# Moving six DMA transposes from the activation queue to the load queue, and the attention steps they feed, in a woven attention and MLP kernel

## The chip, the cores and the metric

The kernel runs on one core of a Trainium2 chip. The metric is the device time of one execution in microseconds (us), the median of several runs. The span in a profile, from the first to the last instruction, is some 1.8 us shorter than the time of the same run. TensorE (PE) multiplies matrices, VectorE (DVE), ScalarE (ACT) and GpSimd (POOL) work element by element, and SyncE (SP) mostly issues DMAs. ACT can issue DMAs too. A run is called slow when it lies over 1.5% above the fastest of its kernel; on one core there is no second die to confirm that, so the label only says that the run was long.

## The reference

The kernel computes, for 4 batches of 768 tokens, a linear attention with a decaying state (8 heads of 64) and then a low rank token mixer and an MLP of 512 to 2048 to 512.

```python
state = gamma * state + k[t] (outer) v[t]          # for each head and token
y[t]  = (q[t] @ state) / sqrt(64)
x     = y as (batch, 768, 512)
u     = x + (xT @ U @ V)T                          # U: 768 x 32, V: 32 x 768
out   = u + max(u @ w_ch1, 0) @ w_ch2              # 512x2048 and 2048x512
```

The recurrence is computed in chunks of 128 tokens: a score block, a causal mask, a mix with the values, and a running state.

## The kernel before

The kernel is one long program in a fixed order. After a prologue (the attention of batch 0) come four MLPs. Into the MLP of batch b−1, PE's main work, the attention of batch b is woven: each small step has a mark, a fraction of the MLP's estimated PE work, and is emitted when that mark is passed. The names in the profile: `in` are loaded tiles (in SBUF, the memory on the chip that the engines work from); POOL casts them to `qd`, `kd`, `vd`; `qT`, `kT` are transposes of pairs of chunks; DVE reorders `qT` to `qO`; a score `s` is kT times qO on PE; `a` is the masked score on DVE; mixes write `o`.

The transposes of batches 2 and 3 are done by DMA, and all loads go out from SP. An engine issues its DMAs one after the other, in the order of the program; I call these its queue. Which engine issues the transposes is this line:

```python
def turn_dma(nm, b, sc):
    (nc.sync if b > 2 else nc.scalar).dma_start_transpose(
        out=turned(nm, b, sc)..., in_=pre[nm, b, sc]...)
```

All loads go out from SP. They are not issued where they are used but 16 tiles ahead: the program starts with 16 loads, and each cast is followed by one further load, of the tile 16 places later in a fixed list.

```python
RING = 16
for _ in range(RING):
    feed_one()                       # nc.sync.dma_start of the next tile
...
def prep_keys(b, keys):
    for key in keys:
        src = take(*key)
        nc.gpsimd.tensor_tensor(t, src, g, op=ALU.mult)   # or tensor_copy for v
        feed_one()
```

The steps of batch 2 (`b == 2`), in the MLP of batch 1:

```python
for sc in range(b == 2, NSC):
    prep_keys(b, pair(b, sc))
if b == 2:
    at = [0.15 + 0.083 * i for i in range(NCK)]       # six chunks
    turns = [None, 0.02, 0.1, 0.19, 0.27, 0.36]       # transposes q k q k q k
lag = [0.0, 0.04, 0.1]                                # state, score, mix
if b == 2:
    for i, f in enumerate(w2_sums(4) + w2_sums(6)):   # differences of w2, DVE
        tracks.append(([f], 0.04 + 0.025 * i, ...))
...
for sc in range(NSC):
    d = at[2 * sc] + lag[1] - 0.02                    # qO just before its score
    tracks.append((q_order(b, sc) on DVE, d, d))
```

The same MLP also gives DVE the "g_sums": sums of halves of the activations `gT`, for a seven product form of the second matmul.

Of the kernel before, what the change touches and what calls it, by code (L numbers as in the profile page):

```python
# [9 lines left out]
fp32 = mybir.dt.float32  # L10
# [8 lines left out]
def kernel(  # L19
# [11 lines left out]
    nc = tc.nc  # L31
# [51 lines left out]
    def evac(eng, dst, src):  # L83
        if eng == "A":
            nc.scalar.activation(dst, src, AF.Copy)  # L85
        else:
            nc.vector.tensor_copy(out=dst, in_=src)  # L87
# [8 lines left out]
    Ub = wts.tile([P, NCK, RK], fp16)  # L96
    V4 = wts.tile([P, S], fp16)
    VR = NSC * RK
    Uf = wts.tile([P, NSC, 2, RK], fp32)
    Vf = wts.tile([VR, SC], fp32)  # L100
    Uh = wts.tile([P, NSC, 2, RK], fp16)
    Vh = wts.tile([VR, SC], fp16)
    w1b = wts.tile([P, NCB, DH], fp16)
    w2b = wts.tile([P, NM, DM], fp16)
    w2t = [wts.tile([P, NH, DQ], fp16, name=f"w2t{i}") for i in range(4)]
# [72 lines left out]
    nc.vector.memset(ones, 1.0)  # L178
    idle_bank = [None]

    def keep_busy(n, fresh=False):
        if fresh:
            idle_bank[0] = bank("mlp")
        for i in range(4 * n):
            nc.tensor.matmul(idle_bank[0][:, ts(i % 4, P)], ones[:, :P],  # L185
                             ones[:, :P], start=True, stop=True,
                             skip_group_check=True)
# [121 lines left out]
    def spread_u():  # L309
        u_p = bank("mlp")  # L310
        for x in range(2):
            for two in range(2):
                nc.tensor.matmul(u_p[ds(HP * two, HP), ds(NSC * RK * x, NSC * RK)],
                                 ident16[:, ds(HP * x, HP)], Uh[:, :, two],
                                 start=(x == 0), stop=True,
                                 skip_group_check=True)
        evac("A", Ub.rearrange("p (s x) r -> p x s r", x=2),
             u_p[:, :NCK * RK].rearrange("p (x s r) -> p x s r", x=2, s=NSC))

    def spread_v():  # L320
        v_p = [bank(t) for t in ("st", "qk")]
        for f in range(NSC):
            nc.tensor.matmul(v_p[f // 2][:, ts(f % 2, SC)], v_sel[:VR, f], Vh,
                             start=(f % 2 == 0), stop=True,
                             skip_group_check=True)
        evac("D", V4[:, :2 * SC], v_p[0])
        evac("A", V4[:, 2 * SC:], v_p[1][:, :SC])

    def prep_w1(mb):
# [105 lines left out]
    def turned(nm, b, sc):  # L435
        if (nm, b, sc) not in live:
            live[nm, b, sc] = rmid.tile([P, 2, 4, P], bf16, tag=nm + "T",
                                        bufs=2, name=f"{nm}T_{b}_{sc}")
        return live[nm, b, sc]

    def q_order(b, sc, src):
# [18 lines left out]
            evac("A", turned(nm, b, sc)[:, r], tp[:, r])  # L460

    def turn_dma(nm, b, sc):
        (nc.sync if b > 2 else nc.scalar).dma_start_transpose(
            out=turned(nm, b, sc).rearrange("p x n m -> p (x n) m"),
            in_=pre[nm, b, sc].rearrange("p x h d -> p (x h d)"))

# [120 lines left out]
    def part(f, *args):  # L587
        return lambda: f(*args)  # L588
# [252 lines left out]
    prep_pair("q", 0, "PD")  # L841
    for sc in range(NSC):
        last = sc + 1 == NSC
        keep_busy(3 if sc else 9, fresh=not last)
        turn_block("k", sc, "D")
        keep_busy(0 if sc else 7)
        turn_block("q", sc, "AD" if last else "A")
        prep_pair("v", sc, "PD" if last else "PA")
        if sc:
            state_half(sc - 1, 1)  # L850
        else:
            keep_busy(4)
        score_block(sc, 0)
        if last:
            prep_uv()
        else:
            prep_pair("k", sc + 1, "PD")
            prep_block("P", "q", sc + 1, 0)
            keep_busy(0 if sc else 3)
        if sc:  # L860
            score_block(sc, 1, "mlp", "DA")
        else:
            score_block(sc, 1)
        if last:
            state_half(sc, 0)
            mix_block(sc - 1, "AD")
            continue
        prep_block("D", "q", sc + 1, 1)
        if sc:
            mix_block(sc - 1, "AA")  # L870
        keep_busy(4 if sc else 1, fresh=sc > 0)
        state_half(sc, 0)
        if sc == 0:
            nc.vector.tensor_scalar(mask, t2.rearrange("p two m -> p (two m)"),
                                    srange, None, op0=ALU.is_ge)
    for mb in range(4):
        prep_w1(mb)
    spread_u()
    for c in range(2):
        x_turn(c, 0)  # L880
    mix_block(NSC - 1, "AD", ("s", "s"))
    spread_v()
    block_stack.close()
    gtp = ctx.enter_context(tc.tile_pool(name="gtp", bufs=1))
    outp = ctx.enter_context(tc.tile_pool(name="outp", bufs=6))
    lr_open(0)
    lr_proj(0)
    for c in range(2):
        x_turn(c, 2)
    for c in range(2, NCB):  # L890
        x_turn(c, 0)
        x_turn(c, 2)
    idle_bank[0] = bank("s")
# [13 lines left out]
    for b in range(1, B + 1):  # L907
# [10 lines left out]
        if b < B:  # L918
            if b == 1:
                at = [0.475, 0.575, 0.63, 0.69, 0.745, 0.8]  # L920
                lag = [0.01, 0.035, 0.065]
                for sc in range(NSC):
                    keys = pair(b, sc)
                    c0, c1 = 2 * sc, 2 * sc + 1
                    if sc:
                        tracks.append(([part(prep_keys, b, keys[:AHEAD])],
                                       at[c0] - 0.1, 1))
                    tracks.append(([part(prep_keys, b, keys[AHEAD:])],
                                   at[c1] - 0.1, 1))
                    for f, d in ((part(turn_pe, "q", b, sc), at[c0] - 0.025),  # L930
                                 (part(turn_pe, "k", b, sc, (0,)), at[c0]),
                                 (part(turn_pe, "k", b, sc, (1,)), at[c1])):
                        tracks.append(([f], d, d))
                tracks.append(([part(prep_keys, 2, pair(2, 0))], at[-1] - 0.04,
                               1))
                tracks.append(([part(turn_dma, "q", 2, 0)], 0.95, 0.95))
                for f, d in zip(w2_sums(0) + w2_sums(2),
                                (0.515, 0.53, 0.55, 0.6, 0.655, 0.67, 0.715,
                                 0.73)):
                    tracks.append(([f], d, d))  # L940
            else:
                for sc in range(b == 2, NSC):
                    prep_keys(b, pair(b, sc))
                if b == 2:
                    at = [0.15 + 0.083 * i for i in range(NCK)]
                    turns = [None, 0.02, 0.1, 0.19, 0.27, 0.36]
                else:
                    at = [0.1 + 0.085 * i for i in range(NCK)]
                    turns = [0.0, 0.04, 0.12, 0.2, 0.28, 0.36]
                lag = [0.0, 0.04, 0.1]  # L950
                if b == 2:
                    for i, f in enumerate(w2_sums(4) + w2_sums(6)):
                        d = 0.04 + 0.025 * i
                        tracks.append(([f], d, d))
                for i, d in enumerate(turns):
                    if d is not None:
                        tracks.append(([part(turn_dma, "qk"[i % 2], b, i // 2)],
                                       d, d))
            if b > 1:
                for sc in range(NSC):  # L960
                    d = at[2 * sc] + lag[1] - 0.02
                    tracks.append(([lambda b=b, sc=sc: q_order(
                        b, sc, live["q", b, sc])], d, d))
            for i in range(NCK):
                for f, d in ((state, lag[0]), (score, lag[1]), (mix, lag[2])):
                    tracks.append(([part(f, b, i)], at[i] + d, at[i] + d))
            t = at[-1] + lag[2]
            if b == 1:
                tracks += [([part(lr_open, b), part(lr_proj, b)], t + 0.02,
                            t + 0.02),  # L970
                           ([part(lr_expand, b, 0, 4)], t + 0.04, t + 0.04),
                           ([part(lr_turn_pair, b, 0, "A"),
                             part(lr_turn_pair, b, 2, "D")], t + 0.08, t + 0.12)]
            else:
                for fs, d in (([part(lr_open, b), part(lr_proj, b)], 0.03),
                              ([part(lr_grow, b, 0, 4, "st")], 0.06),
                              ([part(lr_add, b, 0, 4, (0, 1))], 0.06),
                              ([part(lr_add, b, 0, 4, (2, 3))], 0.11),
                              ([part(lr_turn, b, 0)], 0.17),
                              ([part(lr_turn, b, 2)], 0.171)):  # L980
                    tracks.append((fs, t + d, t + d))
# [30 lines left out]
```

## Time and profile before

| | before |
|---|---|
| time, median of 3 | 234.22 us (233.84 to 234.60) |
| profiled run | 235.99 us, span 234.2 us |
| PE busy | 217.2 us (93%) |
| DVE, ACT, POOL busy | 149.7, 88.1, 84.1 us |

The profile page of the kernel before: busy time and its share of the span by engine, then busy tenths in 40 slices of some 5.9 us, for PE, for its granted clock and for the DMA engines.

```profile
PE 217.2 (93%) x2283; PEld 152.5 (65%) x2283; DVE 149.7 (64%) x303; ACT 88.1 (38%) x186; POOL 84.1 (36%) x120
...
PE   7989799999999999958979999999999999999990
PEclk9999999999999999995999999999999999999997
DMA  5999999999999999999000299910001870000252
```

PE is the bound. Outside the prologue its only dents are slices 18, 19 and 21 (99.5 to 111.2 and 117.1 to 123 us), and in slice 19 its clock is halved. That is the MLP of batch 1, 84.5 to 140.9 us, where batch 2's attention is woven in. DMA is full until 110 us.

Busy time in windows of the kernel before. Columns: window in us, its length; busy us and instructions of PE, PE's weight loads, DVE, ACT, POOL; PE's granted clock; DMA share; GB/s.

```profile
84.50:140.90 56.40, 50.89 (x490) 36.17 (x489) 42.08 (x81) 18.70 (x41) 18.81 (x18) 0.94 0.68 148
102.00:106.30 4.30, 1.04 (x14) 0.63 (x14) 4.15 (x9) 1.68 (x5) 1.95 (x3) 0.89 1.26 227
106.30:112.10 5.80, 5.80 (x35) 3.77 (x36) 2.83 (x5) 1.54 (x4) 0.24 (x1) 0.50 0.74 147
```

In 4.3 us PE has 1.0 us of work while DVE is busy for 4.15; in the 5.8 us after it PE is fully busy at half clock. Of 56.4 us PE is idle for 5.5.

The waits of PE in that stage of the kernel before: who waits for whom, us in total, times, longest.

```profile
PE s L494 <- DVE qO L87: 3.7, 3, 1.8
...
PE o L516 <- DVE a L500: 1.8, 3, 1.2
```

DVE's timeline of the kernel before around the gap. Columns: start, duration, engine, line, operation, output and inputs.

```profile
98.52 1.39 DVE L588 TENSOR_TENSOR gT<-gT 128x768 f16<-128x768 f16 x1
...
100.17 1.06 DVE L588 TENSOR_TENSOR gS<-gT,gS 128x768 f16<-128x768 f16 x1
...
103.67 0.54 DVE L588 TENSOR_TENSOR gS<-gS,gT 128x768 f16<-128x768 f16 x1
...
105.67 0.48 DVE L87 COPY qO<-qT 128x512 bf16<-128x512 bf16 x2
```

The qO copy stands behind g_sums in a DVE queue without gaps. The same instruction form takes 0.54 us alone, and 1.06 to 1.39 us while POOL casts beside it.

The transposes of batch 2 in ACT's timeline of the kernel before:

```profile
82.60 1.33 ACTq L463 DMA_TRANSPOSE qT<-qd  x1
...
98.72 2.32 ACTq L463 DMA_TRANSPOSE qT<-qd  x1
104.63 1.25 ACTq L463 DMA_TRANSPOSE kT<-kd  x1
```

### The profile page before, as it was taken

What the parts mean: (1) busy time and instruction counts of PE and PEld (TensorE: products, weight loads), DVE (VectorE), ACT (ScalarE), POOL (GpSimd) and SP (SyncE); (2) the same over time, 40 slices, a digit from 0 to 9 for tenths busy, and PEclk for the clock granted to TensorE, in tenths of its full rate; (3) what the DMA queues carried; (4) which work ended last, traced back from release to release, by engine and by line L of the source; (5) the groups of instructions that cost most, each with busy time, mean ns of one, the idle gap of its engine ahead of it and who ended that gap; (6) DMA issues with size and microseconds to landing.
All of it is one profiled execution on the core that took longest, in us unless ns stands there. A gap on an engine that the chain in (4) does not pass through costs nothing. (4 is left out here: it accounts for less than half of the span.)

```text
span 234.2 us, 5649 instructions
## 1 busy us (share of the span) xinstructions
PE 217.2 (93%) x2283; PEld 152.5 (65%) x2283; DVE 149.7 (64%) x303; ACT 88.1 (38%) x186; POOL 84.1 (36%) x120
## 2 busy tenths in 40 slices
PE   7989799999999999958979999999999999999990
PEld 7878644684555455635658884556787856668890
DVE  6589456327684575996597844498878443766550
ACT  3267354464653146641712003665510035650000
POOL 5647888978986650470890002000000000000000
PEclk9999999999999999995999999999999999999997
DMA  5999999999999999999000299910001870000252
GB/s 171 338 290 285 277 332 316 391 280 254 228 268 246 261 233 304 263 243 190 0 3 1 50 233 207 234 45 3 3 0 35 190 174 10 1 0 3 68 136 67
DMA packets 84922, 38.84 MB, mean 166 GB/s; under 512 B 58816, under 2 KB 77984, under 8 KB 84896
## 3 DMA queue, kind: packets, MB, share of 16 engines
q1 hardware_dynamic: 77440, 35.27, 58.2%
q10 hardware_dynamic: 7456, 3.21, 6.6%
q8 instruction: 18, 0.29, 0.5%
q14 instruction: 8, 0.07, 0.1%
HBM read 27.46 MB, written 6.29 MB: 144 GB/s over the span
## 5 line engine op out<-in xcount | busy, mean ns | idle before, releaser
L745 PE MATMUL mlp<-uT,w1b 128*128 128x512 f16 (+1 forms) x512 | 91.9, 331 | 0.2 <-DMA uT<-x 0.2
L752 ACT ACTIVATE gT<-mlp 128x512 f16<-128x512 f32 (+1 forms) x94 | 45.2, 490 | 71.5 <-PE mlp L745 51.3
L745 PEld LDWEIGHTS <-w1b 128*128 128x128 f16 x512 | 48.5, 99 | 31.2 <-issue 0.9
L750 DVE TENSOR_SCALAR gT<-mlp 128x512 f16<-128x512 f32 (+1 forms) x34 | 18.9, 555 | 29.2 <-PE mlp L745 29.2
L500 DVE TENSOR_TENSOR a<-s,mask 128x512 bf16<-128x512 f32 x36 | 23.1, 683 | 11.0 <-PE s L494 10.9
L637 PEld LDWEIGHTS <-gT 128*128 128x128 f16 x288 | 27.5, 98 | 3.7
L298 POOL TENSOR_TENSOR kd<-in,gk 128x512 bf16<-128x512 f32 x18 | 19.5, 1087 | 21.0 <-PE st L478 16.8
L790 PE MATMUL mlp<-w2b,gT 128*128 128x512 f16 x96 | 24.1, 380 | 0.0
L637 PEld LDWEIGHTS <-gS 128*128 128x128 f16 x200 | 19.4, 98 | 2.9 <-issue 0.5
L298 POOL TENSOR_TENSOR qd<-in,gq 128x512 bf16<-128x512 f32 x18 | 20.0, 1131 | 3.5 <-DMA in<-in_q_dram 3.5
L296 POOL CAST vd<-in 128x512 bf16<-128x512 f32 x18 | 12.2, 680 | 22.8 <-DMA in<-in_v_dram 19.6
L85 ACT ACTIVATE x<-o 128x512 f16<-128x512 f32 x20 | 11.9, 596 | 21.9 <-PE o L516 21.5
L637 PE MATMUL A<-w2t,gT 128*128 128x256 f16 x144 | 18.5, 273 | 0.0
L85 ACT ACTIVATE state<-st 64x256 bf16<-64x256 f32 x40 | 15.0, 374 | 4.6 <-PE st L374 3.1
L790 PEld LDWEIGHTS <-gT 128*128 128x128 f16 x96 | 8.2, 98 | 7.5
L185 PE MATMUL mlp<-ones 128*128 128x128 bf16 x136 | 10.9, 246 | 1.5 <-DVE ones L178 1.5
L185 PEld LDWEIGHTS <-ones 128*128 128x128 bf16 x148 | 10.3, 111 | 2.1 <-DVE ones L178 1.5
L494 PE MATMUL s<-qO,kT 64*128 64x128 bf16 x144 | 7.4, 223 | 4.1 <-DVE qO L87 3.9
L494 PEld LDWEIGHTS <-kT 64*128 64x128 bf16 x144 | 4.4, 96 | 9.8 <-issue 5.6
L331 POOL CAST w1b<-in 128x512 f16<-128x512 f32 x16 | 9.5, 612 | 1.9 <-DMA in<-in_moe_w_ch_dram 1.5
L516 PE MATMUL o<-vd,a 128*128 128x64 bf16 x144 | 8.1, 195 | 2.1 <-DVE a L500 2.1
L337 POOL CAST w2b<-in 128x512 f16<-128x512 f32 x16 | 9.6, 613 | 1.0 <-DMA in<-in_moe_w_ch_dram 0.5
(143 smaller groups left out, 285.2 us busy)
## 6 DMA issues: line engine op xcount, KB each, us to landing
in<-in_moe_w_ch_dram SPq DMA_DIRECT2D x32, 256.0 KB, 5.2
in<-in_k_dram SPq DMA_DIRECT2D x24, 256.0 KB, 4.8
in<-in_q_dram SPq DMA_DIRECT2D x24, 256.0 KB, 4.5
in<-in_v_dram SPq DMA_DIRECT2D x24, 256.0 KB, 4.9
out_dram<-o SPq DMA_DIRECT2D x32, 128.0 KB, 2.4
out_dram<-o ACTq DMA_DIRECT2D x12, 128.0 KB, 3.9
out_dram<-o SPq DMA_DIRECT2D x6, 64.0 KB, 2.1
Uf<-in_moe_U_dram SPq DMA_DIRECT2D x1, 96.0 KB, 5.1
```

The source lines that it names most:

```text
L85: nc.scalar.activation(dst, src, AF.Copy)
L185: nc.tensor.matmul(idle_bank[0][:, ts(i % 4, P)], ones[:, :P], ones[:, :P], start=True, stop=True, skip_group_check=True)
L296: nc.gpsimd.tensor_copy(out=t, in_=src)
L298: nc.gpsimd.tensor_tensor(t, src, g, op=ALU.mult)
L337: nc.gpsimd.tensor_copy(out=w2b[:, m], in_=take("w2", m))
L494: nc.tensor.matmul(sp[h % 2][:, ts(h // 2, P)], kT[r, h // 2], qT[r, h // 2], start=True, stop=True)
L500: nc.vector.tensor_tensor(a, four(sp[i]), causal(mask), op=ALU.mult)
L637: nc.tensor.matmul(acc[key, i], lhs[:, m, ts(i, P)], rhs[:, m], start=(fresh and m == 0), stop=(m == NH - 1), skip_group_check=True)
L745: nc.tensor.matmul(g_p[:, :sz], w1b[:, c, ts(m, P)], uTs[b][:, ds(j, nj), c], start=(c == 0), stop=(c == NCB - 1))
L750: nc.vector.tensor_relu(gT[:, m, ds(lo, sz)], g_p[:, :sz])
L752: nc.scalar.activation(gT[:, m, ds(lo, sz)], g_p[:, :sz], AF.Relu)
L790: nc.tensor.matmul(ch, gT[:, m, ts(j, P)], w2b[:, m], start=(m == 0), stop=(m == NM - 1))
```

## The change

The intent: issue the six transposes of batch 2 from SP right behind the casts that they read, during the MLP of batch 0, so that their results are there early; then start batch 2's steps earlier in the MLP (0.04 instead of 0.15) and spread them wider (0.10 instead of 0.083), out of the crowded part of DVE's queue. In each pair k is now transposed before q; before it was q, then k. One mark of batch 1's query transposes moves by 0.01 (left out below). In the prologue, the work on U and V and the turns of x are reordered, one DVE copy goes to ACT, and some narrow idle matmuls become fewer wide ones.

The diff, cut to its core:

```diff
@@ turned
-                                        bufs=2, ...
+                                        bufs=2 + (nm == "k"), ...
@@ turn_dma
-        (nc.sync if b > 2 else nc.scalar).dma_start_transpose(
+        nc.sync.dma_start_transpose(
@@ prologue (cut)
-        evac("D", V4[:, :2 * SC], v_p[0])
+        evac("A", V4[:, :2 * SC], v_p[0])
...
+            u_p = spread_u()
             state_half(sc, 0)
+            hold_u(u_p)
...
-    spread_u()
-    for c in range(2):
-        x_turn(c, 0)
     mix_block(NSC - 1, "AD", ("s", "s"))
     spread_v()
+    x_turn(0, 0)
+    x_turn(0, 2)
@@ MLP of batch 0: casts and transposes of batch 2
-                tracks.append(([part(prep_keys, 2, pair(2, 0))], at[-1] - 0.04, 1))
-                tracks.append(([part(turn_dma, "q", 2, 0)], 0.95, 0.95))
+                for sc in range(NSC):
+                    keys, d = pair(2, sc), at[-1] - 0.04 + 0.06 * sc
+                    for fs in ([part(prep_keys, 2, keys[:2])],
+                               [part(turn_dma, "k", 2, sc)],
+                               [part(prep_keys, 2, keys[2:4])],
+                               [part(turn_dma, "q", 2, sc)],
+                               [part(prep_keys, 2, keys[4:])]):
+                        tracks.append((fs, d, d))
@@ MLP of batch 1: steps of batch 2
-                if b == 2:
-                    at = [0.15 + 0.083 * i for i in range(NCK)]
-                    turns = [None, 0.02, 0.1, 0.19, 0.27, 0.36]
+                at = [(0.04, 0.1)[b - 2] + (0.1, 0.085)[b - 2] * i
+                      for i in range(NCK)]
```

More of the change, by code (lines that the diff above doesn't have):

```diff
@@ L98 @@
     VR = NSC * RK
-    Uf = wts.tile([P, NSC, 2, RK], fp32)
-    Vf = wts.tile([VR, SC], fp32)
-    Uh = wts.tile([P, NSC, 2, RK], fp16)
-    Vh = wts.tile([VR, SC], fp16)
+    Uf = blk.tile([P, NSC, 2, RK], fp32, bufs=1)
+    Vf = blk.tile([VR, SC], fp32, bufs=1)
+    Uh = blk.tile([P, NSC, 2, RK], fp16, bufs=1)
+    Vh = blk.tile([VR, SC], fp16, bufs=1)
     w1b = wts.tile([P, NCB, DH], fp16)
@@ L179, with keep_busy @@
     idle_bank = [None]
-    def keep_busy(n, fresh=False):
+    def keep_busy(n, fresh=False, wide=False):
         if fresh:
             idle_bank[0] = bank("mlp")
+        if wide:
+            for i in range(n):
+                nc.tensor.matmul(idle_bank[0], ones[:, :P], ones, start=True,
+                                 stop=True, skip_group_check=True)
+            return
         for i in range(4 * n):
@@ L316, in spread_u, with hold_u @@
                                  skip_group_check=True)
+        return u_p
+    def hold_u(u_p):
         evac("A", Ub.rearrange("p (s x) r -> p x s r", x=2),
@@ L437, in turned @@
             live[nm, b, sc] = rmid.tile([P, 2, 4, P], bf16, tag=nm + "T",
-                                        bufs=2, name=f"{nm}T_{b}_{sc}")
+                                        bufs=2 + (nm == "k"), name=f"{nm}T_{b}_{sc}")
         return live[nm, b, sc]
@@ L843 @@
         last = sc + 1 == NSC
-        keep_busy(3 if sc else 9, fresh=not last)
+        keep_busy(3 if sc else 9, fresh=not last, wide=not sc)
         turn_block("k", sc, "D")
@@ L887 @@
     lr_proj(0)
-    for c in range(2):
-        x_turn(c, 2)
-    for c in range(2, NCB):
+    for c in range(1, NCB):
         x_turn(c, 0)
@@ L929 @@
                                    at[c1] - 0.1, 1))
-                    for f, d in ((part(turn_pe, "q", b, sc), at[c0] - 0.025),
+                    for f, d in ((part(turn_pe, "q", b, sc), at[c0] - 0.035),
                                  (part(turn_pe, "k", b, sc, (0,)), at[c0]),
@@ L933 @@
                         tracks.append(([f], d, d))
-                tracks.append(([part(prep_keys, 2, pair(2, 0))], at[-1] - 0.04,
-                               1))
-                tracks.append(([part(turn_dma, "q", 2, 0)], 0.95, 0.95))
+                for sc in range(NSC):
[6 more added lines that the diff above has]
+                        tracks.append((fs, d, d))
                 for f, d in zip(w2_sums(0) + w2_sums(2),
@@ L941 @@
             else:
-                for sc in range(b == 2, NSC):
-                    prep_keys(b, pair(b, sc))
-                if b == 2:
-                    at = [0.15 + 0.083 * i for i in range(NCK)]
-                    turns = [None, 0.02, 0.1, 0.19, 0.27, 0.36]
-                else:
-                    at = [0.1 + 0.085 * i for i in range(NCK)]
-                    turns = [0.0, 0.04, 0.12, 0.2, 0.28, 0.36]
+                if b > 2:
+                    for sc in range(NSC):
+                        prep_keys(b, pair(b, sc))
+                    for i, d in enumerate((0.0, 0.04, 0.12, 0.2, 0.28, 0.36)):
+                        tracks.append(([part(turn_dma, "qk"[i % 2], b, i // 2)],
+                                       d, d))
+                at = [(0.04, 0.1)[b - 2] + (0.1, 0.085)[b - 2] * i
+                      for i in range(NCK)]
                 lag = [0.0, 0.04, 0.1]
@@ L954 @@
                         tracks.append(([f], d, d))
-                for i, d in enumerate(turns):
-                    if d is not None:
-                        tracks.append(([part(turn_dma, "qk"[i % 2], b, i // 2)],
-                                       d, d))
             if b > 1:
```

## The prediction

> **What bounds the kernel now.** TensorE (PE). The page shows PE busy 217.2 of 234.2 us, DVE 149.7, ACT 88.1, POOL 84.1; only PE's idle time, and time at half clock, can be won. Busy time in windows of one microsecond shows where: (a) prologue, to 29 us, several gaps, 1.2 us of them between 25 and 28 us; (b) the MLP of batch 1, in which batch 2's attention is woven (84 to 138 us): 0.65 us at 94, 3.3 us between 102.0 and 106.3, 1.3 us at 118, 0.3 us at 122.7, some 5.5 us in all; (c) the granted clock is 0.50 from 105.3 to 112.1 us, directly after that gap. PE is busy for 5.8 us of it at half speed: some 2.9 us more. The Trainium skill (TensorE: Matmul & The Clock Gate, Part 1) says that an idle window of about 3.4 us halves the clock; the trace agrees: 1.0 us of work in 4 us, then 0.50.
>
> **Why PE idles in (b).** The waits view charges 3.9 us to score matmuls (L494) waiting for DVE's reordered queries qO, and 2.1 us to mixes (L516) waiting for the masked scores. The timeline shows the later qO at 105.67 and 117.30 us, in a DVE queue without gaps: differences of w2, then the g_sums (0.54 us alone, 1.06 to 1.43 us while POOL casts batch 3 beside them). At 94 us, qO waited for its transpose. Batch 2's casts are done at 86.6 us, but its six transposes, in order in ACT's queue, go out at 82.6, 85.6, 90.5, 93.6, 98.7 and 104.6 us.
>
> **What the change does.** The six transposes (1.25 to 1.34 us of issue each, 5 us to land) go out from SP right behind the casts, which end at 67 to 84 us; I estimate landings between 75 and 97 us, the third q last, since its buffer waits for qO of the first pair. DMA is full (share 1.0 to 1.25) from 2 to 110 us, so they push loads back by about 3 us each, but loads of batches 2 and 3, needed later. ACT loses six issue stalls. Steps start at 0.04 of the MLP instead of 0.15 and are 0.10 apart instead of 0.083: score 1 comes before the first g_sums. No work leaves PE; DVE loses one copy (0.68 us). The prologue drops a DVE copy ahead of pc, fills a wait with U, and moves x turns; 36 narrow idle matmuls become 9 wide ones of equal time. All this: 0.5 us.
>
> **Sum.** Of the 5.5 us of idle PE I expect 3.5 us back; DVE stays crowded between 0.22 and 0.30 and near 0.46 of the MLP (g_sums before qO). Half clock: 2.9 us in the profiled execution, a slow one (235.99 against 234.22 us), so I count 1.7 us for the timed ones. Prologue 0.5. Total 5.7 us: **228.5 us**, 8 in 10 between 225.8 and 232.0. Faster by over 2%: 0.60; within: 0.37; slower: 0.03.
>
> **What would show it.** Right: granted clock 1.00 throughout 84 to 140 us; L494 waiting for qO under 2 us; batch 2's transposes issued on SP before 92 us; PE idle in that stage about 2 us; the first L745 matmul about 0.5 us earlier than 29.4 us. Wrong: qO still late with DVE busy before it (then DVE's order counts, not the transposes), or POOL waiting for loads and qO for transposes near 100 us.
>
> **What would make it wrong.** Timed runs that never had the half clock (gain nearer 4 us); POOL's batch 3 casts, starting earlier, slowing the same DVE instructions; SP blocked at the third q transpose, holding batch 3's loads; a new stall in batch 1's stage from shifted q turns.

## The result and the profile after

The changed kernel takes 242.01 us (median of 4: 242.5, 241.52, 246.31, labelled slow, and 240.62), against 234.15 us of the kernel before in the same rounds. The ratio is 1.031, with a 95% interval of 1.026 to 1.037: slower. A ratio here is the mean time of one kernel's fast runs over that of the other's of the same rounds, so it is not quite the ratio of the medians. Results were correct here and in all runs below. In the profile after, line numbers have moved by 8: score matmuls are L502, up matmuls L753, transposes L471, mixes L524. In the experiments that hold loads back they have moved by 14.

The profile page of the kernel after, the lines that answer to those of before:

```profile
PE 220.5 (92%) x2256; PEld 150.9 (63%) x2256; DVE 146.6 (61%) x302; ACT 89.0 (37%) x187; POOL 82.9 (34%) x120
...
PE   7989999999999973978959999999999999999992
PEclk9999999999999997797979999999999999999999
DMA  6999999999999999999300079960000784000163
```

PE has three dents now, in slices 15 and 16, 18 and 19, and 21 (84 to 96, 102 to 114 and 120 to 126 us), and a lower clock in or behind each. To find the stage that lost, I take for each profiled run the start of the first up matmul of each batch (and the last matmul); the differences are the stages, in us:

| | prologue | MLP 0 | MLP 1 (attention of batch 2 woven in) | MLP 2 | MLP 3 |
|---|---|---|---|---|---|
| before | 29.4 | 55.1 | 56.4 | 48.4 | 39.3 |
| after | 28.7 | 55.5 | 64.0 | 48.5 | 39.4 |

The whole loss, 7.6 us, lies in the MLP of batch 1. (The profiled run of before was one of its longer ones, labelled slow, with the same dents as above; against a typical run of before the loss is rather larger than that.) Busy time in windows of the kernel after: the stage, and each gap with what follows it.

```profile
84.20:148.20 64.00, 53.71 (x490) 36.46 (x489) 41.00 (x80) 19.24 (x41) 19.76 (x20) 0.89 0.71 145
89.00:94.20 5.20, 0.62 (x9) 0.53 (x8) 0.54 (x3) 1.02 (x1) 0.19 (x1) 0.86 1.05 193
94.20:99.80 5.60, 5.59 (x24) 2.23 (x23) 3.08 (x7) 1.19 (x2) 0.00 (x0) 0.52 1.15 244
106.80:109.00 2.20, 0.03 (x1) 0.01 (x1) 2.20 (x7) 0.60 (x1) 0.00 (x0) 1.00 1.06 182
109.00:114.00 5.00, 4.98 (x29) 2.22 (x30) 2.72 (x6) 1.19 (x2) 0.00 (x0) 0.66 1.20 194
120.80:123.30 2.50, 0.00 (x1) 0.01 (x1) 2.50 (x4) 0.00 (x0) 2.50 (x3) 1.00 0.00 0
123.30:127.00 3.70, 3.68 (x24) 2.62 (x25) 2.39 (x4) 1.15 (x3) 2.09 (x2) 0.54 0.00 0
```

The first gap is a new kind: from 89 to 94.2 us PE, DVE, ACT and POOL all have next to nothing to do, and only DMA is busy. In the second and third gap DVE is busy for every microsecond while PE waits, as in the gap of the kernel before. After each gap the clock is halved for a time. Idle PE in the stage rose from 5.5 to 10.3 us (64.0 − 53.7), and busy PE from 50.9 to 53.7 us for the same 490 matmuls, which fits the lower clock. DVE's timeline of the kernel after, ahead of the second and of the third gap's end:

```profile
107.92 0.55 DVE L596 TENSOR_TENSOR gS<-gT,gS 128x768 f16<-128x768 f16 x1
108.39 0.49 DVE L87 COPY qO<-qT 128x512 bf16<-128x512 bf16 x2
...
120.12 0.96 DVE L596 TENSOR_TENSOR gT<-gT 128x768 f16<-128x768 f16 x1
121.00 2.17 DVE L87 COPY qO<-qT 128x512 bf16<-128x512 bf16 x2
```

The qO copies stand behind g_sums, as in the kernel before.

The waits of the kernel after in this stage:

```profile
PE s L502 <- DVE qO L87: 9.3, 3, 4.6
...
DVE qO L87 <- DMA qT<-qd: 6.4, 1, 6.4
```

PE's wait for qO went from 3.7 to 9.3 us. DVE in its turn waited 6.4 us for one transpose. The chain is in these timelines of the kernel after. POOL's casts of the first pair:

```profile
67.59 2.04 POOL L303 TENSOR_TENSOR kd<-in,gk 128x512 bf16<-128x512 f32 x2 [0.48 <-PE qk L461]
69.59 2.23 POOL L303 TENSOR_TENSOR qd<-in,gq 128x512 bf16<-128x512 f32 x2
```

SP's queue:

```profile
73.18 1.13 SPq L153 DMA_DIRECT2D in<-in_q_dram  x2
74.40 2.46 SPq L153 DMA_DIRECT2D in<-in_v_dram  x2
76.95 2.55 SPq L153 DMA_DIRECT2D in<-in_k_dram  x2
...
85.16 2.11 SPq L471 DMA_TRANSPOSE kT<-kd  x1
87.37 1.28 SPq L153 DMA_DIRECT2D in<-in_k_dram  x2
88.71 2.88 SPq L471 DMA_TRANSPOSE qT<-qd  x1
```

DVE, then PE (in brackets: idle time before the instruction, and what ended it):

```profile
93.66 0.49 DVE L87 COPY qO<-qT 128x512 bf16<-128x512 bf16 x2 [6.41 <-DMA qT<-qd]
```

```profile
94.21 0.61 PE L502 MATMUL s<-qO,kT 64*128 64x128 bf16 x8 [4.59 <-DVE qO L87]
```

The keys `kd` of the first pair are cast at 69.6 us and the queries at 71.8, but SP issues their transposes at 85.16 and 88.71, 15.5 and 16.9 us later. Between 71.3 and 85.2 us SP issued, one right behind the other, ten loads and six stores that stand before the transpose in its order; issuing one took it 0.5 to 1.9 us, all sixteen 12.4 us. The other four go out at 94.03, 98.23, 104.50 and 108.61, 17.8, 18.3, 20.7 and 21.8 us behind their casts. The step that needs the first one was meanwhile moved forward. The trace alone doesn't tell how much of the loss is the late transposes, how much the early steps, how much DVE's order, and how much the clock. The experiments take these apart, the clock's share only roughly.

### The profile page after: what moved, and what is told of

Its sections match the earlier page's. It is cut to its first block, busy times and chain, and to the rows that moved or that the text cites. A ratio compares the mean times of both kernels' runs of the same rounds, so it can differ in the third digit from the quotient of the medians.

```text
span 240.7 us, 5594 instructions
## 1 busy us (share of the span) xinstructions
PE 220.5 (92%) x2256; PEld 150.9 (63%) x2256; DVE 146.6 (61%) x302; ACT 89.0 (37%) x187; POOL 82.9 (34%) x120
## 4 chain that ended last, share of the span: by engine, by line
PE 55%; DMA 24%; DVE 10%; POOL 5%; ACT 2%; issue 2%; ACTq 0%; SPq 0%; POOLq 0%; DVEq 0%
PE mlp L753 22%; PE A L645 13%; DMA in<-in_k_dram 9%; DMA in<-in_v_dram 7%; PE C L645 5%; DMA in<-in_moe_w_ch_dram 4%; PE B L645 3%; DVE gS L596 3%; DMA qT<-qd 2%; DMA in<-in_q_dram 2%; PE s L502 2%; POOL w1b L339 2%; PE mlp L186 2%; PE mlp L190 2%; DVE x L561 2%
## 5 line engine op out<-in xcount | busy, mean ns | idle before, releaser
L753 PE MATMUL mlp<-uT,w1b 128*128 128x512 f16 (+1 forms) x512 | 95.0, 340 | 0.6 <-ACT gT L760 0.6
L753 PEld LDWEIGHTS <-w1b 128*128 128x128 f16 x512 | 49.8, 101 | 34.8 <-issue 6.4
L303 POOL TENSOR_TENSOR qd<-in,gq 128x512 bf16<-128x512 f32 x18 | 19.3, 1091 | 2.6 <-DMA in<-in_q_dram 2.6
L502 PE MATMUL s<-qO,kT 64*128 64x128 bf16 x144 | 7.5, 225 | 9.5 <-DVE qO L87 9.5
L502 PEld LDWEIGHTS <-kT 64*128 64x128 bf16 x144 | 4.4, 96 | 15.3 <-issue 12.3
L561 DVE TENSOR_TENSOR x<-s,x 128x256 f16<-128x256 f32 (+1 forms) x16 | 8.1, 549 | 3.7 <-ACT gT L760 2.1
L645 PE MATMUL B<-w2b,gT 128*128 128x256 f16 x72 | 9.4, 273 | 0.0
L645 PE MATMUL A<-w2b,gT 128*128 128x256 f16 x72 | 9.2, 273 | 0.0
```

Of the source, the lines that this page charges most:

```text
L502: nc.tensor.matmul(sp[h % 2][:, ts(h // 2, P)], kT[r, h // 2], qT[r, h // 2], start=True, stop=True)
L561: nc.vector.tensor_tensor(us[b][:, ds(j0, nj), ts(c, P)], four(grown[b][c])[:, :nj], xs[b][:, ds(j0, nj), ts(c, P)], op=ALU.add)
L645: nc.tensor.matmul(acc[key, i], lhs[:, m, ts(i, P)], rhs[:, m], start=(fresh and m == 0), stop=(m == NH - 1), skip_group_check=True)
L753: nc.tensor.matmul(g_p[:, :sz], w1b[:, c, ts(m, P)], uTs[b][:, ds(j, nj), c], start=(c == 0), stop=(c == NCB - 1))
```

## The experiments

Theory A (backlog): the transposes' place in SP's queue is the cause. The loads go out 16 tiles ahead while DMA is full (share 1.08 from 60 to 84 us), so a transpose "right behind the cast" stands behind a backlog of loads. Theory B (marks): the earlier marks are the cause, whatever the queue. Theory C (DVE's order): qO stands behind w2 differences and g_sums. Theory D (clock): the gaps alone are small, and the half clock makes the loss. In each experiment the kernel before ran in the same rounds on the same chip. Times are medians of 4 runs unless said otherwise.

### Parts alone

**e2: the prologue alone.** The prologue of after, everything else of before. Expected:

> The kernel before with only the prologue part of the change (wide idle matmuls, U spread early, V copies on ACT, x turns moved, U and V in the block pool); batch 2 exactly as before. Backlog theory (the loss comes from batch 2's transposes standing behind a backlog of loads in SP's queue): the prologue is harmless, first MLP matmul near 28.7 us instead of 29.4, time 233.3 to 234.2 us. Rival (the reordered prologue shifts everything after it into a worse phase): 237 us or more.

Measured: 238.61 us (235.56, 238.66, 238.56, 238.76), ratio 1.022 [1.012, 1.033]. This is a miss: the time lies in the rival's range. The prologue itself ended at 28.0 us instead of 29.4. But ACT stood still later. ACT's timeline of e2:

```profile
94.25 1.31 ACTq L471 DMA_TRANSPOSE qT<-qd  x1
95.61 1.09 ACT L760 ACTIVATE gT<-mlp 128x512 f16<-128x512 f32 x2 [5.43 <-issue]
```

ACT did nothing for 5.4 us ahead of issuing a transpose, its activations behind it were late, and PE's up matmuls waited 4.5 us for them. The trace lists the semaphores (counters on which engines wait) of each instruction. This transpose waits for a completion semaphore that SP and ACT both use, and that a load of `in_k`, issued by SP at 86.93 us, had used last; the load landed at 94.17 us and the wait ended at 94.19. That explains the wait in the profiled run (235.56 us); the three timed runs are 3 us longer and have no trace. Run e11 returns to this.

**e5: batch 2's part alone.** The prologue of before, everything else of after.

> The kernel before with only the batch 2 part (transposes on SP behind the casts, steps from 0.04 with 0.10 between, third kT buffer). Backlog theory: all of the loss is here: 241 to 243 us, kT of the first pair issued some 15 us after its cast, qO waits for the q transpose near 90 us. Rival (prologue): 234 to 236 us.

Measured: 242.17 us (one run slow), ratio 1.039 [1.033, 1.045]; the MLP of batch 1 took 64.2 us, as in after (64.0). The loss belongs to batch 2's part: it is all there with the old prologue. So in the changed kernel the new prologue adds nothing to it that shows, although alone (e2) it cost 2.2%.

**e3: after with the old marks.**

```diff
-                at = [(0.04, 0.1)[b - 2] + (0.1, 0.085)[b - 2] * i
+                at = [(0.15, 0.1)[b - 2] + (0.083, 0.085)[b - 2] * i
```

> The changed kernel with only the marks of batch 2's steps put back (0.15 and 0.083 apart); transposes stay on SP. Backlog theory: the transposes are issued as late as in the changed kernel (85 to 109 us), but the first score comes some 4 us later in PE's order, so the 4.6 us gap at 90 us shrinks to 1 us or less; 236 to 239 us. Rival A (SP's queue alone is to blame, need and mark do not matter): 241 us or more. Rival B (the order of steps alone is to blame): 233 to 234.5 us.

Measured: 233.50 us, ratio 1.002 [0.993, 1.011]; stage 54.9 us. The transposes were still issued on SP, at 85.6 to 108.8 us, as late as in after, but PE's scores waited only 1.7 us for qO, against 9.3. The time misses the range of the backlog theory and falls into rival B's: by this run alone the marks are to blame, and with the old marks the late transposes cost nothing that shows. That the backlog counts has to come from the runs below.

**e9: before with the new marks only**, transposes on ACT as before.

```diff
-                    at = [0.15 + 0.083 * i for i in range(NCK)]
+                    at = [0.04 + 0.1 * i for i in range(NCK)]
```

> The kernel before with only the marks of batch 2's steps changed (0.04, 0.10 apart); transposes on ACT at their old marks, issued between 82 and 105 us. Backlog theory (early need meets late transposes, whatever queue they stand in): the first score waits some 1 to 3 us, the later ones for transposes at marks 0.19 and 0.36 against needs at 0.28 and 0.48; MLP stage of batch 1 at 55 to 60 us, 233 to 238 us, between the two kernels. Rival A (the steps alone are to blame): stage at 63 to 65 us, 241 us. Rival B (SP alone is to blame): stage below 54 us, under 231 us.

Measured: 237.88 us, ratio 1.020 [1.010, 1.031]. As expected. The score's wait for qO was 4.7 us, and there was a gap at 115 us with half clock behind it.

These runs cross marks and queue, though not cleanly: SP's side also has the casts in batch 0's MLP and the third buffer of kT. The new marks cost 2.0% with ACT's queue and 2.9% (after against e3: 1.031 against 1.002) with SP's. The marks are harmful by themselves (B). The two costs are not clear of each other, as the intervals of e9 and after overlap. But e5, which has the prologue of e9, lies clear above it (1.033 to 1.045 against 1.010 to 1.031): with the new marks SP's side costs more.

### The backlog

**e4: nine tiles ahead instead of sixteen.** `RING = 9`, otherwise after.

> The changed kernel with a load ring of 9 tiles instead of 16, so that at most one load beyond the eight in flight stands in SP's queue ahead of a transpose. Backlog theory: kT of the first pair is issued some 8 us after its cast instead of 15.6 (seven loads of about 1.07 us fewer ahead of it), at 76 to 80 us, qO no longer waits for it, the gap at 90 us is gone; 231 to 236 us if the loads are not starved elsewhere. Rival (the order of DVE's work in the MLP of batch 1, not the transposes): 239 to 242 us, the gaps stay.

Measured: 239.87 us (one slow), ratio 1.026 [1.020, 1.032]. The transposes were issued at 77.44 to 100.04 us, some 8 us earlier than in after, and the first gap was gone. The MLP of batch 1 fell from 64.0 to 54.2 us. But the MLP of batch 2 rose from 48.5 to 56.3: POOL waited 26.7 us for a load of batch 3, and its queries and keys came late. The shorter ring moved loads to behind later work in SP's queue, the transposes of u, which went out at 130.5 us. So the stage confirmed what the test was made for, and the time of the whole shows none of it: it missed the 231 to 236 us and lies in the rival's range.

**e6: seven loads held back and given later.** Ring of 16; at the start of batch 0's MLP the next seven calls for a load do nothing, and the seven are issued behind the last transpose of batch 2.

```diff
     def feed_one():
+        if held_back[0]:
+            held_back[0] -= 1
+            held_back[1] += 1
+            return
...
             if b == 1:
+                held_back[0] = 7
...
+                    if sc == NSC - 1:
+                        tracks.append(([lambda: [feed_one() for _ in
+                                       range(held_back[1])]], d, d))
```

> The changed kernel, but seven loads are held back from the start of batch 1's stage and issued right after the last of batch 2's transposes: the ring acts as one of 9 only while the transposes go out, and batch 3's loads are not pushed behind the uT transposes as with the ring of 9. Backlog theory: kT of the first pair issued near 77 us, MLP stage of batch 1 near 54 us as with the ring of 9 (64.0 in the changed kernel), MLP stage of batch 2 back at 48.5 us (56.3 with the ring of 9); 231 to 234 us. Rival (the ring of 9 helped that stage by something else than the transposes' place in the queue): 237 us or more.

Measured: 236.40 us (one slow), ratio 1.011 [0.996, 1.026]; stage 58.5 us, and the MLP of batch 2 kept its 49.4. Time and stage lie above what was expected, though under the rival's 237 us. SP's timeline of e6:

```profile
77.60 2.12 SPq L477 DMA_TRANSPOSE kT<-kd  x1
...
81.08 2.10 SPq L477 DMA_TRANSPOSE qT<-qd  x1
```

The first transpose goes out 7.6 us earlier than in after (85.16), for seven loads taken from before it. A load of 256 KB takes some 1.1 us at the 233 GB/s that DMA moved between 60 and 84 us in after (my estimate), seven take some 8. That is theory A by its number, and the other five transposes moved by 7.2 to 8.3 us as well. But a gap of 4 us was left, from 98.3 to 102.3 us, and one of 2.5 us at 114. DVE's timeline and then PE's of e6:

```profile
98.53 1.39 DVE L602 TENSOR_TENSOR gT<-gT 128x768 f16<-128x768 f16 x1
...
100.18 1.15 DVE L602 TENSOR_TENSOR gS<-gT,gS 128x768 f16<-128x768 f16 x1
101.25 0.90 DVE L87 COPY qO<-qT 128x512 bf16<-128x512 bf16 x2
```

```profile
102.29 0.40 PE L508 MATMUL s<-qO,kT 64*128 64x128 bf16 x8 [4.01 <-DVE qO L87]
```

The transposed queries had landed; qO has no wait for DMA. It stands behind the g_sums. That is theory C.

**e7: e6, and qO earlier in DVE's order.**

```diff
-                    d = at[2 * sc] + lag[1] - 0.02
+                    d = at[2 * sc] + lag[1] - 0.02 - (0.07 if b == 2 and sc else 0)
```

> As the held-back kernel, and the reordering copies of queries (qO) of the second and third pair are moved up by 0.07 of the MLP in DVE's order, ahead of differences of w2 and g_sums. If what is left of the loss is DVE's order (qO at 102.6 us behind g_sums with DVE busy all the time, in the ring of 9), its 3 us gap and the half clock after it vanish: MLP stage of batch 1 at 49 to 51 us, 227 to 230.5 us, better than both kernels. If it is the transposes that are still late, DVE now stands still for them and the time is 232 us or more.

Measured: 232.81 us (232.40 to 233.09), ratio 0.999 [0.991, 1.006]; stage 53.3 us, granted clock 1.000 in the profiled run. This misses the 227 to 230.5 us and the stage of 49 to 51. The cause named for a miss, DVE standing still for late transposes, was small: DVE waited 0.7 us for one. PE waited 0.2 us for qO. With the backlog shortened and qO moved ahead, the loss of the change is gone with its new marks still in place. What was left were mixes waiting 2.4 us for the masked scores, again in DVE's queue.

### The clock

**e8: idle matmuls ahead of three scores.** After, with eight wide matmuls of no use before the score of chunks 0, 2 and 4 of batch 2.

```diff
         sp = [bank("s") for _ in range(2)]
+        for _ in range(8 if b == 2 and ci % 2 == 0 else 0):
+            nc.tensor.matmul(sp[0], ones[:, :P], ones, start=True, stop=True, ...)
```

> The changed kernel with eight wide idle matmuls (1.7 us at full clock) ahead of the first score of each pair of batch 2, in the gaps where PE waits for qO; no wait is removed. Theory that about half of the loss is the clock that halves after a gap: each remaining gap (2.9, 0.5, 0.8 us) is too short, the granted clock stays at 1.00 from 84 to 130 us, and 4 to 7 us come back: 235 to 238 us. Rival (the waits alone cost the time): 241 to 243 us.

Measured: 239.75 us, ratio 1.029 [1.017, 1.041]; stage 60.5 us against 64.0. A miss: the time lies between the two ranges, and the ratio is not clear of after's 1.031, so what the clock is worth can be read from the two profiled stages only. Busy time in windows of e8: the first gap that is left, and what follows.

```profile
91.00:94.90 3.90, 0.01 (x1) 0.09 (x1) 0.38 (x2) 0.00 (x0) 0.00 (x0) 0.96 1.26 246
94.90:98.00 3.10, 2.93 (x14) 1.23 (x14) 3.10 (x8) 0.46 (x1) 0.00 (x0) 0.50 1.29 245
```

This gap, 4.1 us in all (to 95.1 us), is still followed by half clock. Behind the other two, shortened, the clock stayed at full. The mean clock of the stage rose from 0.89 to 0.97. So the clock's share of the loss seems to be a few microseconds (3.5 us of stage here, one run each), in line with the trace of after, where PE's busy time in the stage was 2.8 us above before's. The waiting itself stays: by these traces D is an addition to the loss, not its cause.

### Can the idea be made to pay?

**e10: e7, and the second half of the w2 differences in the MLP of batch 0** (marks 0.76 to 0.865 there), out of DVE's crowded stretch.

> The held-back kernel with qO moved up, and the eight differences of w2 that DVE does in the MLP stage of batch 1 (3.4 us alone, more beside POOL) moved into the stage before, where DVE is busy about half of the time around 72 to 80 us. If DVE is what PE still waits for in that stage (53.3 us; mixes wait 2.4 us for masked scores, downs 1.2 us), the stage takes 50.5 to 52.5 us, the stage before stays within 0.7 us of 55.9 us: 229.5 to 232 us, 1 to 2% under the kernel before. Rival (DVE's load no longer matters once qO is early): 232.5 us or more.

Measured, 6 runs: 232.06 us (230.84 to 232.14), ratio 0.994 [0.989, 0.998]; stage 53.0 us, where 50.5 to 52.5 was expected: a miss. Taking the w2 differences out bought hardly anything over e7 (53.3).

**e11: e2 with the seven loads held back.** If e2's stall of ACT came from transposes that wait for loads in SP's backlog, a shorter backlog should remove it.

> The prologue part of the change alone (238.6 us, against 232 to 237 of the kernel before) with seven loads held back while batch 2's transposes go out on ACT at their old marks. Theory: ACT's transposes also wait for loads that stand in SP's backlog (in the prologue-only kernel ACT stood 5.4 us before the second q transpose, issued at 94.25 us, and PE waited 4.5 us for an ACT copy); with a short backlog ACT no longer stands, no PE wait for ACT's copies over 1.5 us, 230.5 to 233.5 us with little spread. Rival (the prologue itself slows batch 2's stage): 236 us or more.

Measured: 233.28 us (232.73 to 233.52), ratio 1.000 [0.994, 1.006]. As expected: ACT's stall is gone and the spread is small. The transposes stay on ACT here, so ACT's queue is no escape from the backlog: it can wait for loads of SP's, as the semaphore in e2's trace shows. That this also is what made e2's timed runs long is supported, not proven, since they have no trace and the held loads moved other transfers too.

**e12: e10 with the old marks.**

```diff
-                at = [(0.04, 0.1)[b - 2] + (0.1, 0.085)[b - 2] * i
+                at = [(0.15, 0.1)[b - 2] + (0.083, 0.085)[b - 2] * i
```

> As e10, with the step marks of the kernel before (0.15, 0.083 apart). If the wider, earlier steps are good once transposes and DVE are out of the way, this is slower than e10 by 1 to 3 us, its MLP stage of batch 1 at 52 to 55 us. If the earlier steps bring nothing, it is equal to e10 or faster.

Measured, 6 runs: 227.03, 234.29, 231.99, 228.68, 232.13, 231.69 us; median 231.84 against 233.04 of the kernel before. The profiled run was the best of the six. Busy time in windows of e12, the MLP of batch 1:

```profile
83.20:132.40 49.20, 48.10 (x489) 34.58 (x488) 38.08 (x73) 18.94 (x41) 22.82 (x23) 1.00 0.98 193
```

In that run PE had 1.1 us of idle time in the stage and a full clock. But the other runs are up to 7 us longer. By the 1.5% rule four of the six count as slow, so the ratio of fast runs, 0.977 [0.969, 0.985], rests on the two best. The means of all runs give 0.989 (230.97 against 233.42 us). I take the second for what the kernel is worth: about 1%, and no better in the median than e10 (232.06), so within this spread the earlier steps bring nothing. Why its runs differ is open; their mean clocks (0.988 to 1.000) don't order them: the longest run had 0.999.

**e13: e12 without holding the loads back.** One line removed, `held_back[0] = 7`. Transposes, old marks and w2 order stay.

> As e12 (old step marks, qO moved up, w2 differences in the stage before), but no loads held back: batch 2's transposes again stand behind the full backlog of SP's queue and go out between 85 and 109 us. Backlog theory: with qO moved up by 0.07 in DVE's order DVE now stands still for the late q transposes of the second and third pair; MLP stage of batch 1 at 53 us or more (49.2 in e12), best runs 231 us or more. Rival (with the old marks the place of the transposes in the queue does not matter, DVE's order did it all): stage at 49 to 50.5 us, best runs at 227 to 229 us as in e12.

Measured, 6 runs: 234.32 us, ratio 1.005 [0.998, 1.011]; all runs' means 0.998 (234.18 against 234.77 us). DVE's timeline of e13:

```profile
113.57 1.76 DVE L87 COPY qO<-qT 128x512 bf16<-128x512 bf16 x2 [2.91 <-DMA qT<-qd]
```

With the full backlog the last transpose goes out at 109.27 us (101.68 in e12) and DVE waits 2.9 us for it (0.3 in e12). So the backlog matters for the third pair even with the old marks. Stage and best run (232.61 us) are as the backlog theory expected. In means of all runs the hold is worth about 0.8% (0.989 against 0.998), which is hardly clear of e12's spread and less than the 5.2 us between the two profiled stages (54.4 and 49.2), since e12's profile shows its best run.

### The runs together

| run | marks | transposes from | loads held | qO early | w2 early | stage, us | median, us | ratio |
|---|---|---|---|---|---|---|---|---|
| before | old | ACT | no | no | no | 56.4 | 234.15 | 1 |
| e9 | new | ACT | no | no | no | 56.3 | 237.88 | 1.020 |
| after | new | SP | no | no | no | 64.0 | 242.01 | 1.031 |
| e3 | old | SP | no | no | no | 54.9 | 233.50 | 1.002 |
| e6 | new | SP | yes | no | no | 58.5 | 236.40 | 1.011 |
| e7 | new | SP | yes | yes | no | 53.3 | 232.81 | 0.999 |
| e10 | new | SP | yes | yes | yes | 53.0 | 232.06 | 0.994 |
| e12 | old | SP | yes | yes | yes | 49.2 (its best run) | 231.84 | 0.977, all runs 0.989 |
| e13 | old | SP | no | yes | yes | 54.4 | 234.32 | 1.005 |

Stages are of the profiled run, one for each kernel. The profiled run of before was one of its longer ones (235.99 us), and that of e9 its shortest (236.40), which is why e9's stage looks no longer than before's while its median is.

## Why the prediction was wrong

The prediction was 228.5 us, 225.8 to 232.0; the result 242.01. It was wrong in sign.

1. **The step that failed first**: "The six transposes ... go out from SP right behind the casts, which end at 67 to 84 us; I estimate landings between 75 and 97 us". They were emitted right behind the casts in the program, but issued 15.5 to 21.8 us after them (85.16 to 108.61 us) and landed between 91.0 and 114.0 us, since SP's in order queue held loads and stores first, ten and six of them before the first transpose. The prediction counted what the transposes would do to the loads ("push loads back by about 3 us each") and not what the loads would do to the transposes. SP's timeline of the kernel before had the material: loads go out about one every 1.1 to 1.3 us without a break, and the program has them 16 tiles ahead. e6 confirms the mechanism by its size: seven loads fewer, 7.6 us earlier. The Trainium skill (DMA: Bandwidth & Descriptors, Rules for kernel authors) says that spreading DMAs over queues doesn't help bandwidth and only saves issue time on the sequencer. The traces agree on bandwidth, the share being above 1.0 with either queue. But the issue times of the DMAs ahead add up in an in order queue: sixteen of them put the first transpose 15.5 us behind its cast.

2. **The second failing step**: "Steps start at 0.04 ... score 1 comes before the first g_sums" was counted as gain. Alone (e9) the new marks cost 2.0%, and with them taken out (e3) the loss of the change is gone. The move made the first need of qO fall at 89.6 us, where the transposes could not be, and it did not take the later copies of qO out from behind the g_sums: at 120.8 us in after, and 4 us in e6, PE waited for qO with DVE busy all the time. So of the 5.5 us of idle PE, 3.5 were to come back, and 4.8 were added (10.3).

3. **The clock** was expected at 1.00 through the stage ("granted clock 1.00 throughout 84 to 140 us"). It was halved behind three gaps. The Trainium skill (TensorE: Matmul & The Clock Gate, Part 1) gives an idle window of about 3.4 us for that. Behind 4.6 us in after and 4.1 us in e8 the trace agrees; behind gaps of 2.2 and 2.5 us in after the clock was halved as well, so gaps below the rule of thumb are not safe. In the kernel before it was halved behind gaps of 1.2 and 1.8 us with 1.3 us of work between them, so the prediction's "the trace agrees" was a loose fit. Where 1.7 us were to come back, PE's busy time in the stage grew by 2.8 us, some 3 of the 7.6.

4. **What was right.** DVE's order as a reason why PE waits; e7 shows it for the changed kernel, by moving the copies of two pairs. For the kernel before it is read from the timeline; no run moved qO alone there. The sign "qO still late with DVE busy before it (then DVE's order counts, not the transposes)" was named, and it came for the second and third gap, and "qO for transposes near 100 us" for the first. The prologue's 0.5 us is neither confirmed nor refuted: the first up matmul came 0.7 us earlier (28.7 against 29.4), but e5 and e9, which have the old prologue, had it at 28.4 and 30.4. POOL beside DVE: the Trainium skill (SBUF — State Buffer, SBUF: two separate sides) describes a port pair that DVE instructions with two SBUF inputs and GpSimd instructions take exclusively; here the g_sums took 0.54 us alone and mostly 1.06 to 1.43 us beside POOL's casts, which fits, though it does not tell an exclusive pair from a shared one.

5. **The range and the chances.** "Slower by over 2%" got 0.03. The last paragraph of the prediction named "SP blocked at the third q transpose" and a new stall from shifted turns, but treated the queue as empty otherwise. A range that took the start of the transposes as uncertain by 16 loads would have been open on the slow side.

What stays open: the spread of e12 (227.0 to 234.3 us), and of the kernel before, between 231 and 239 us over all rounds; the 3 us between e2's profiled and timed runs; and why e10's stage, with its w2 differences out of the way, gained only 0.3 us on e7's. The cheapest test of DVE's order, qO earlier in the kernel before and nothing else, was not run. Batch 2's transposes on ACT at after's places were not run: with a third buffer for qT, put in so that ACT would not block at the third transpose, the program does not build, as its tiles no longer fit in SBUF.

## What to carry to other kernels

When a transfer is moved to another queue, read in the trace how far that queue runs ahead: count what stands before it in program order, times the time each takes to go out, and only then say when it lands. Do not move the consumer earlier in the same edit unless that time allows it; and where a busy in order engine (here DVE) feeds PE, move the copy that PE waits for ahead in that engine's order, which was worth 3.6 us of median here (e6 to e7). A local gain has to be followed to the end of the program: the shorter ring won 9.8 us in one stage and gave back 7.8 in the next.

## What the Trainium skill lacked or had wrong

- TensorE: Matmul & The Clock Gate, Part 1 (HAM oscillation): the rule of "no PE-idle gaps" above some 3.4 us is not safe from below. Gaps of 2.2 us (106.8 to 109.0, PE busy without a break before it) and 2.5 us (120.8 to 123.3) were followed by a clock of 0.66 and 0.54 over the next 5.0 and 3.7 us. The length alone does not decide: behind a gap of 2.2 us in e9 (102.4 to 104.6) the clock stayed full.
- DMA: Bandwidth & Descriptors, Rules for kernel authors: spreading DMAs over engines is described as saving sequencer time only. The rules lack how that time adds up when loads are issued ahead: 15.5 to 21.8 us between cast and issue of a transpose, and 7.6 us less for seven loads fewer.
- DMA: Bandwidth & Descriptors gives the sequencer's time for a DMA transpose only in a table that compares trn3 with earlier chips, for other shapes. Here issuing one took 1.2 to 1.4 us on ACT's queue in most cases (up to 3.0), and 1.2 to 4.1 us on SP's.
- No page gives the cost of completion semaphores that two issuing engines share: in e2 ACT's own work stood still for 5.4 us ahead of a transpose whose semaphore belonged to a load of SP's.
